# A hold behind the silu step in the build-time plan of a fused attention and SwiGLU kernel

## The chip, the cores and the metric

The kernel runs on one core of a Trainium2 chip. The core has a matrix engine (TensorE, PE in the profile, with its weight loads as PEld), a vector engine (VectorE, DVE), a scalar engine (ScalarE, ACT), GpSimd (POOL) and SyncE (SP), which here only issues DMAs. Each engine takes its own instructions strictly in the order in which they were emitted and waits on semaphores of the others. The metric is the device time of one execution in microseconds (us), less is better. The time before is the median of three runs, 379.68 us (379.57 to 379.87).

## The reference

Causal attention with a forget gate (64 heads of 576 tokens, 64 wide), whose output is laid out as 4608 tokens of 512, followed by a SwiGLU feed-forward block with 1536 hidden columns:

```python
scores = q @ k.T / sqrt(64) + (cum[:, None] - cum[None, :])   # cum = cumsum(log(clip(f, 1e-4, 1)))
attn   = softmax(where(causal, -1e9, scores))
x      = (attn @ v) -> (4608, 512)
g      = x @ w_gate
out    = (g * sigmoid(g) * (x @ w_val)) @ w_out
```

Inputs and output are float32; the kernel computes its matmuls in bf16.

## The kernel before

The kernel is not written as a fixed sequence. Every step (a matmul group, an activation, a DMA) is first recorded as an `Op` with its engine, an estimated duration, its predecessors, the buffers that it takes and releases, and a key. `Plan.run` then simulates the five engines at build time: whenever an engine is free, it takes the ready step with the smallest key whose buffers can be had, emits its instructions there and then, and moves that engine's clock on by the estimated duration. The order in which steps are emitted is the order in every engine's queue on the chip, DMA queues among them; the estimated times themselves are not in the program, only the order. So an estimate that changes by a tenth of a microsecond can let another step be the ready one, and from there on all queues may differ.

When a step ends in the plan, three events are pushed. The engine is free at `busy[e]`. Steps that can run only on the same engine learn of it at `busy[e]` too; steps of other engines learn of it later by `PIPE[e]` (0.12 us for VectorE, 0.2 for TensorE):

```python
o.done = end + self.PIPE[e]
push(busy[e], "wake", None)
push(o.done, "end", o)
push(busy[e], "done", (o, e, True))
push(o.done, "done", (o, e, False))
```

The attention part handles a pair of heads at a time: scores on TensorE (`score`, line 704), exponentials on ScalarE (`expo`, 738), the causal mask on GpSimd (`mask`, 747), weighing by V on TensorE (`weigh`, 761), then on VectorE the reciprocal of the row sums (`invert`, 768) and the scaling (`scale`, 773). A scaled pair goes into `xT`, through TensorE and a VectorE copy or by a DMA transpose on SP's queue (`cross`, 791). One PSUM bank ("o") holds the weighed sums of a head; the next head's weighing takes it when the scaling has released it. Loads of later batches are paced by fixed release times.

The feed-forward part runs over twelve token tiles, `TILES = (512, 512, 128) * 4` in effect, and in a 512-token tile over twelve blocks of 128 hidden columns. One such unit (`unit`, line 1057) is: gate matmuls into a bank (`gate`, 919), tanh on ScalarE (`tanh`, 930), silu on VectorE (`silu`, 940: (tanh + 1) times the gate bank, written to a `th` buffer), value matmuls into a second bank (919 with `wv`), and the product on VectorE (`times`, 943: `th` times the value bank, written to `hh`). Silu releases the gate bank, the product the value bank; four banks ("f") serve the feed-forward part until 290 us in the plan. A 128-token tile does the same for four blocks at once (`ffn1`, line 1099; `gate4` 926, `times4` 947, `pairs` 952, which sums what `times4` wrote). From tile 8 on, ScalarE computes silu by itself (`whole`, 933), and no VectorE silu exists: 82 of them run in tiles 0 to 7.

The products of a 512-token tile are summed in pairs on VectorE (`sums`, 976, three steps for each pair of blocks) and multiplied by the output weights with seven products in place of eight (`product`, 985); the weights' own sums are made once (`blend`, 964). The results go through ScalarE, GpSimd and VectorE (1011, 1018, 1022, 1043, 1046) into `ot` and to memory. The first tile uses a plain multiplication (`project`, 992), 128-token tiles `single` (998).

Keys decide among ready steps: tanh, silu, product and `pairs` have -5, attention steps some hundreds and thousands, feed-forward matmuls 100000 and more for each tile, the sums 50000 and the weights' sums 40000. A table `ORDER` overrides the keys of the steps numbered 0 to 596 and 1521 to 1580 (with gaps): the loads and the decay rows, the first batches of attention, and the first units of tile 0. Among steps with one key, the one recorded first goes first.

Of the kernel before, what the change touches and what calls it, by code (L numbers as in the profile page):

```python
# [34 lines left out]
class Plan:  # L35
# [9 lines left out]
    def op(self, eng, fn, after=(), behind=(), take=(), use=(), key=0.0, ready=0.0, dma=None):  # L45
        o = Op(eng, fn, list(after), behind, list(take), list(use), key, ready, dma)
        for b in o.use:
            b.left += 1
        self.ops.append(o)
        return o  # L50
# [26 lines left out]
    def run(self, idle=None):  # L77
# [9 lines left out]
        busy = {e: 0.0 for e in engines}  # L87
# [5 lines left out]
        left, t, seq = len(self.ops), 0.0, 0  # L93
        events = []

        def push(at, kind, o):
            nonlocal seq
            seq += 1
            heapq.heappush(events, (at, seq, kind, o))
# [9 lines left out]
        while left:  # L109
# [3 lines left out]
            t = events[0][0]  # L113
            while events and events[0][0] <= t + 1e-9:
                _, _, kind, o = heapq.heappop(events)
                if kind in ("queue", "dma"):
                    for r, share in shares():
                        r[0][0] -= (t - moved) * share
                        while r and r[0][0] < 1e-6:
                            over, n = r.pop(0)  # L120
# [27 lines left out]
                elif kind == "done":  # L148
                    o, e, own = o
# [6 lines left out]
            for e in engines:  # L156
                while busy[e] <= t + 1e-9:
                    k = kind_of.get(e)
                    full = k and lanes[k][taken[k] % 8] > t
                    if e == "SP" and full:  # L160
                        break
                    ready[e] = [o for o in ready[e] if o.start is None]
                    best = None
                    for o in sorted(ready[e], key=lambda o: (o.key, o.n)):
                        if o.dma is not None and full:
                            continue
                        if self._takes(o, t):
                            best = o
                            break
                    if best is None:  # L170
                        break
                    o = best
                    o.start, o.ran = t, e
                    dur = o.eng[e]
                    if e == "PE":
                        dur *= self.clock(t)
                        self._fill(idle, busy[e], t)
                    o.fn(e)
                    busy[e] = end = t + dur
                    for s in o.then:  # L180
                        s.wait -= 1
                        if not s.wait:
                            push(max(t, s.ready), "ready", s)
                    if o.dma is not None:
                        o.lane = taken[k] % 8
                        lanes[k][o.lane] = 1e9
                        taken[k] += 1
                        push(max(end + (0.53 if o.tag == "f" else 0.9), T_SW if e == "POOL" else 0.0), "queue", o)
                        push(busy[e], "wake", None)
                    else:  # L190
                        o.done = end + self.PIPE[e]
                        push(busy[e], "wake", None)
                        push(o.done, "end", o)
                        push(busy[e], "done", (o, e, True))
                        push(o.done, "done", (o, e, False))
        return max(o.done for o in self.ops)

# [24 lines left out]
def kernel(ctx, tc, q, k, v, f, w_gate, w_val, w_out, out):  # L222
# [11 lines left out]
    MT = 512  # L234
# [67 lines left out]
        lambda t: 2.0 if t < TWARM else 1.0,  # L302
    )

    def op(eng, fn, *args, tag=None, packet=20.0, **kw):
        if not isinstance(eng, dict):
            eng = {eng[0]: eng[1]}
        o = plan.op(eng, lambda e: fn(e, *args), **kw)
        o.tag, o.packet = tag, packet
        return o  # L310

    E = {"ACT": nc.scalar, "DVE": nc.vector, "POOL": nc.gpsimd, "SP": nc.sync, "PE": nc.tensor}
# [1 line left out]
    def act(n):  # L314
        return 0.055 + n / 1200

    def dve(n, psum=True):
        return (n + (75 if psum else 58)) / 960

    def mm(*cols):  # L320
        return sum(c / 2400 + 0.0025 for c in cols)
# [147 lines left out]
    def blank(e, what):  # L469
# [46 lines left out]
        else:  # L516
            if what != "rest":
                fill32(e, VB[what][:, :, :, D:].bitcast(F32), ONE2)
            if what:
# [4 lines left out]
              after=[op(("DVE", 0.07), lambda e: nc.vector.memset(warm, 1.0), key=-30)])  # L524
# [532 lines left out]
    def unit(t, fc, t0, n, hs, lo, kk, after):  # L1057
        if (t, fc) == ALONE:
            tabled.append(op(("ACT", 1.4), turn_table, after=before + exps, key=-6, tag="table"))
        needs = [o for a, b, done in x_ready.values() if a < t0 + n and b > t0 for o in done]  # L1060
        wr = [w_ready["g", fc // FCG], w_ready["v", fc // FCG]]
        bg, bv, bt = Buf(*F_POOLS(t)), Buf(*F_POOLS(t)), Buf("th")
        p, r = divmod(fc, 2)
        fresh = hs[p] is None
        if fresh:
            hs[p] = Buf("hh")
            hs[p].first = None
        g = op(("PE", mm(*[n] * KD)), gate, wg, fc, t0, n, bg, after=needs + wr + after, behind=[] if fresh else [hs[p].gate], take=[bg] + ([hs[p]] if fresh else []), key=kk, tag=("gp", t, fc))
        if fresh:
            hs[p].gate = g  # L1070
        alone = (t, fc) >= ALONE
        if alone:
            b = op(("ACT", act(n)), whole, n, bg, bt, after=[g] + tabled, take=[bt], use=[bg], key=-5, tag=("tanh", t, fc))
        else:
            b = op(("ACT", act(n)), tanh, n, bg, bt, after=[g], take=[bt], use=[bg], key=-5, tag=("tanh", t, fc))
            before.append(b)
            b = op(("DVE", dve(n)), silu, n, bg, bt, after=[b], use=[bg, bt], key=-5, tag=("silu", t, fc))
        a = op(("PE", mm(*[n] * KD)), gate, wv, fc, t0, n, bv, after=[g], take=[bv], key=kk + 1, tag=("vp", t, fc))
        m = op(("DVE", dve(n)), times, n, bv, bt, hs[p], r, lo, 1.0 if alone else 0.5, after=[a, b, hs[p].first],
               use=[bv, bt, hs[p]], key=-5, tag=("mul", t, fc))  # L1080
        if fresh:
            hs[p].first = m
        read.append((t0, t0 + n, [g, a]))
        return g, m
# [14 lines left out]
    def ffn1(t, t0):  # L1099
        key, bn, ms, first = 1e5 * (t + 1), Buf("nh"), [], []  # L1100
        for fq in range(KF // 4):
            if (t, 4 * fq) == ALONE:
                tabled.append(op(("ACT", 1.4), turn_table, after=before + exps, key=-6, tag="table"))
            needs = [o for a, b, done in x_ready.values() if a < t0 + P and b > t0 for o in done]
            wr = [w_ready[n, c] for n in "gv" for c in range(4 * fq // FCG, (4 * fq + 3) // FCG + 1)]
            bg, bv, bt = Buf(*F_POOLS(t)), Buf(*F_POOLS(t)), Buf("th")
            kk = key + 400 * fq
            g = op(("PE", mm(*[P] * 4 * KD)), gate4, wg, fq, t0, bg, after=needs + wr + [last_gate[0]], behind=first, take=[bg] + ([] if fq else [bn]), key=kk, tag=("gp", t, 4 * fq))
            first = first or [g]
            alone = (t, 4 * fq) >= ALONE  # L1110
            if alone:
                b = op(("ACT", act(MT)), whole, MT, bg, bt, after=[g] + tabled, take=[bt], use=[bg], key=-5, tag=("tanh", t, 4 * fq))
            else:
                b = op(("ACT", act(MT)), tanh, MT, bg, bt, after=[g], take=[bt], use=[bg], key=-5, tag=("tanh", t, 4 * fq))
                before.append(b)
                b = op(("DVE", dve(MT)), silu, MT, bg, bt, after=[b], use=[bg, bt], key=-5, tag=("silu", t, 4 * fq))
            a = op(("PE", mm(*[P] * 4 * KD)), gate4, wv, fq, t0, bv, after=[g], take=[bv], key=kk + 1, tag=("vp", t, 4 * fq))
            m = op(("DVE", dve(MT)), times4, fq, bv, bt, 1.0 if alone else 0.5, after=[a, b] + first, use=[bv, bt, bn], key=-5, tag=("mul", t, 4 * fq))
            ms.append(op({"DVE": fast(HALF)}, pairs, fq, after=[m], use=[bn], key=-5, tag=("pairs", t, fq)))
            read.append((t0, t0 + P, [g, a]))  # L1120
        last_gate[0] = g
        tails.append((t, t0, key, bn, ms))
# [129 lines left out]
    t0 = 0  # L1252
    for t, n in enumerate(TILES):
        ffn(t, t0, n) if n == MT else ffn1(t, t0)
        t0 += n
    for r in tails[:QUICK]:
        simple(*r)
    ready = [w_ready["o", c] for c in range(NCO)]
    blended = [op({e: f((KF // 2) * HALF // 2) + 0.35 * (n // 2 == 1) for e, f in BLEND_ON.items()}, blend, n, after=ready, key=BLEND_KEY + n, ready=BLEND_AT, tag=("blend", n)) for n in range(6)]
    blended += [op({e: f((KF // 2) * HALF // 2) for e, f in BLEND_ON.items()}, blend, n, after=blended[:6] + plain, key=BLEND_KEY + n, ready=BLEND_AT, tag=("blend", n)) for n in range(6, 10)]  # L1260
    for r in tails[QUICK:]:
        (finish if TILES[r[0]] == MT else lone)(*r, blended)

# [16 lines left out]


QUICK = 1
TILES = (512, 512, 128) * 3 + (512, 512, 128)


def F_POOLS(t):
    return ("f",) + tuple((x, WIDE_AT, 1e9) for x in "sot")
# [152 lines left out]
```

## Time and profile before

| | |
|---|---|
| median of three runs | 379.68 us |
| the profiled execution | 379.88 us |
| its span, first to last instruction | 378.1 us |
| granted TensorE clock | 1.000 |
| VectorE busy | 259.9 us |
| ScalarE busy | 213.3 us |
| GpSimd busy | 168.6 us |

In the profile, "L940" is line 940 of the kernel. A row of instructions in order of time gives the start, the duration, engine, line, operation, output and inputs with their shapes; a bracket at its end gives how long the engine had been idle before it and whose result ended that. A matmul's end is modelled, so a short wait of TensorE between two matmuls does not show as idle time. "th", "hh", "su", "nh", "ps" are the tiles of those names with their buffer numbers left out.

### The profile page before, as it was taken

What the parts mean: (1) busy time and instruction counts of PE and PEld (TensorE: products, weight loads), DVE (VectorE), ACT (ScalarE), POOL (GpSimd) and SP (SyncE); (2) the same over time, 40 slices, a digit from 0 to 9 for tenths busy, and PEclk for the clock granted to TensorE, in tenths of its full rate; (3) what the DMA queues carried; (4) which work ended last, traced back from release to release, by engine and by line L of the source; (5) the groups of instructions that cost most, each with busy time, mean ns of one, the idle gap of its engine ahead of it and who ended that gap; (6) DMA issues with size and microseconds to landing.
All of it is one profiled execution on the core that took longest, in us unless ns stands there. A gap on an engine that the chain in (4) does not pass through costs nothing.

```text
span 378.1 us, 9696 instructions
## 1 busy us (share of the span) xinstructions
PE 369.3 (98%) x3715; PEld 248.7 (66%) x3715; DVE 259.9 (69%) x605; ACT 213.3 (56%) x436; POOL 168.6 (45%) x396
## 2 busy tenths in 40 slices
PE   8899999999999999999999999999999999999996
PEld 5667655455679655775468965578666964584596
DVE  7879886499947699538983669854889246717633
ACT  7899953265646544766477465757775223323322
POOL 8897544135656243695058632656440400040021
PEclk9999999999999999999999999999999999999999
DMA  8999998895949998999969999497730120011012
GB/s 149 189 198 196 206 209 157 178 199 102 167 84 215 172 193 159 142 201 209 187 127 181 203 239 202 88 179 174 146 37 19 57 83 2 1 56 57 0 54 88
DMA packets 125179, 52.04 MB, mean 138 GB/s; under 512 B 111838, under 2 KB 119582, under 8 KB 124366
## 3 DMA queue, kind: packets, MB, share of 16 engines
q1 hardware_dynamic: 108638, 36.15, 48.7%
q0 software_dynamic: 16288, 15.14, 26.3%
q8 instruction: 29, 0.48, 0.5%
q10 hardware_dynamic: 208, 0.14, 0.1%
q14 instruction: 16, 0.13, 0.1%
HBM read 38.56 MB, written 17.07 MB: 147 GB/s over the span
## 4 chain that ended last, share of the span: by engine, by line
PE 87%; DVE 6%; DMA 2%; ACT 2%; issue 1%; POOL 0%; DVEq 0%; ACTq 0%; POOLq 0%
PE ps L919 40%; PE ps L985 16%; PE ps L704 9%; PE ps L761 8%; PE ps L926 5%; PE ps L998 3%; PE ps L992 3%; DVE hh L943 2%; DVE su L976 2%; DMA su<-in_q_dram 1%; DVE th L940 1%; DMA natv<-in_v_dram 1%; DVE xn L773 1%; PE ps L722 1%; PE ps L778 1%
## 5 line engine op out<-in xcount | busy, mean ns | idle before, releaser
L738 ACT ACTIVATE PT<-ps 128x384 bf16<-128x384 f32 (+2 forms) x192 | 90.9, 510 | 19.1 <-PE ps L704 12.6
L919 PE MATMUL ps<-xT,wv 128*128 128x512 bf16 (+1 forms) x400 | 99.3, 370 | 0.0
L919 PE MATMUL ps<-xT,wg 128*128 128x512 bf16 (+1 forms) x400 | 99.1, 370 | 0.0
L943 DVE SCALAR_TENSOR_TENSOR hh<-th,ps 128x512 bf16<-128x512 f32 (+1 forms) x100 | 66.2, 664 | 23.3 <-PE ps L919 16.3
L930 ACT ACTIVATE th<-ps 128x512 f32<-128x512 f32 (+1 forms) x82 | 47.2, 577 | 52.0 <-PE ps L919 45.1
L747 POOL TENSOR_SCALAR_AFFINE_SELECT PT<-PT 128x128 bf16<-128x128 bf16 (+1 forms) x192 | 53.7, 288 | 42.2 <-ACT PT L738 37.0
L704 PE MATMUL ps<-QK 68*128 68x256 bf16 x392 | 63.0, 261 | 0.0
L919 PEld LDWEIGHTS <-wg 128*128 128x128 bf16 x400 | 37.7, 97 | 34.5
L919 PEld LDWEIGHTS <-wv 128*128 128x128 bf16 x400 | 37.5, 97 | 34.5
L940 DVE SCALAR_TENSOR_TENSOR th<-th,ps 128x512 f32<-128x512 f32 (+1 forms) x82 | 53.5, 653 | 9.2 <-ACT th L930 8.8
L747 POOL TENSOR_SCALAR_AFFINE_SELECT PTa<-PTa 128x256 bf16<-128x256 bf16 x64 | 26.7, 419 | 69.6 <-ACT PTa L738 68.3
L976 DVE TENSOR_TENSOR su<-hh 128x512 bf16<-128x512 bf16 (+1 forms) x126 | 46.6, 413 | 1.1
L985 PEld LDWEIGHTS <-su 128*128 128x128 bf16 x420 | 40.1, 98 | 5.5 <-DVE su L976 0.4
L761 PE MATMUL ps<-VB,PT 128*128 128x65 bf16 x768 | 41.9, 193 | 0.0
L704 PEld LDWEIGHTS <-QK 68*128 68x128 bf16 x392 | 31.3, 97 | 12.9 <-ACT QK L328 0.2
L761 PEld LDWEIGHTS <-PT 128*128 128x128 bf16 x768 | 34.7, 97 | 7.5 <-POOL PT L747 0.6
L1018 POOL TENSOR_TENSOR ot<-ot 128x256 f32<-128x256 f32 x14 | 10.1, 722 | 63.7 <-ACT ot L1011 63.7
L933 ACT ACTIVATE th<-ps 128x512 f32<-128x512 f32 x30 | 17.9, 596 | 33.1 <-PE ps L919 27.7
L738 ACT ACTIVATE PTa<-ps 128x384 bf16<-128x384 f32 x64 | 30.9, 488 | 9.9 <-PE ps L704 8.7
L768 DVE RECIPROCAL rc<-ps 128x5 f32<-128x5 f32 (+2 forms) x68 | 12.7, 187 | 31.0 <-PE ps L761 30.8
L773 DVE TENSOR_TENSOR xn<-ps,rc 128x320 bf16<-128x320 f32 (+2 forms) x72 | 32.4, 453 | 2.2
L985 PE MATMUL ps<-wt,su 128*128 128x256 bf16 x252 | 33.2, 272 | 0.2 <-DVE su L976 0.2
(101 smaller groups left out, 410.4 us busy)
## 6 DMA issues: line engine op xcount, KB each, us to landing
out_dram<-ot SPq DMA_DIRECT2D x35, 256.0 KB
natv<-in_v_dram SPq DMA_DIRECT2D x25, 256.0 KB
qk_d<-in_q_dram POOLq DMA_DIRECT2D x24, 144.0 KB, 3.7
qk_d<-in_k_dram POOLq DMA_DIRECT2D x24, 144.0 KB, 4.7
wv<-in_moe_w_val_dram POOLq DMA_DIRECT2D x3, 512.0 KB, 9.8
wg<-in_moe_w_gate_dram POOLq DMA_DIRECT2D x3, 512.0 KB, 12.3
wo<-in_moe_w_out_dram POOLq DMA_DIRECT2D x4, 384.0 KB, 13.7
VB<-in_v_dram POOLq DMA_DIRECT2D x7, 128.0 KB, 10.0
```

The source lines that it names most:

```text
L704: nc.tensor.matmul(s[:, c : c + w], QK[:KR, hqk[p].i, 1, j * S + kt * P : j * S + (kt + 1) * P], QK[:KR, hqk[p].i, 0, j * S + q0 : j * S + ...
L738: nc.scalar.activation(place(h, i)[:, OFFS[i] : OFFS[i] + c], ps(bs)[:, :c], AF.Exp, scale=0.125)
L747: nc.gpsimd.affine_select(out=d, in_=d, pattern=pat, compare_op=ALU.is_ge, fill=0.0, base=0, channel_multiplier=-1,)
L761: nc.tensor.matmul(o[:, lo : lo + D + 1], pt[:, c : c + P], VB[hvb[b].i][:, kt, hb, : D + 1], start=first and n == 0, stop=last and n == l ...
L773: nc.vector.tensor_mul(XN[bx.i][:, qb : qb + nq, j], o, r)
L919: nc.tensor.matmul(ps(bf)[:, a:b], w[:, ko, fc * P : (fc + 1) * P], xT[:, ko, at : at + b - a], start=ko == 0 and a == 0, stop=ko == KD - ...
L926: nc.tensor.matmul(ps(bf)[:, c * P : (c + 1) * P], w[:, ko, (4 * fq + c) * P : (4 * fq + c + 1) * P], xT[:, ko, lo : lo + P], start=c + ko ...
L930: nc.scalar.activation(TH[bt.i][:, :n], ps(bf)[:, :n], AF.Tanh, scale=0.5)
L940: nc.vector.scalar_tensor_tensor(out=t, in0=t, scalar=1.0, in1=ps(bf)[:, :n], op0=ALU.add, op1=ALU.mult)
L943: nc.vector.scalar_tensor_tensor(out=HH[bh.i][:, r, lo : lo + n], in0=TH[bt.i][:, :n], scalar=by, in1=ps(bf)[:, :n], op0=ALU.mult, op1=ALU ...
L976: E[e].tensor_tensor(out=o, in0=x, in1=y, op=f)
L985: nc.tensor.matmul(ps(bf)[:, c * HALF : (c + 1) * HALF], left(g)[:, q * P : (q + 1) * P], right[:, g], start=opens and g == 0, stop=g == K ...
```

## The change

`op` takes a further argument, `raw`, 0 by default, and keeps it on the step. In `Plan.run`, the event that tells steps of the same engine of a step's end is pushed later by that amount; the engine itself is free when it was, and steps of other engines and buffers are told when they were. The two silu steps get `raw=RAW` with `RAW = 0.17`, and the product of the 128-token tiles gets `raw=0.1`. The product of the 512-token tiles, the reciprocal and all others keep 0. Keys, estimated durations, buffers and the computation of every step stay as they are. The instructions are the same; their order in the queues comes out of a plan in which a VectorE step that reads silu's result becomes ready 0.17 us behind silu's end, and `pairs` 0.1 us behind its product's.

```diff
@@ -191,7 +191,7 @@
                         o.done = end + self.PIPE[e]
                         push(busy[e], "wake", None)
                         push(o.done, "end", o)
-                        push(busy[e], "done", (o, e, True))
+                        push(busy[e] + o.raw, "done", (o, e, True))
                         push(o.done, "done", (o, e, False))
@@ -302,11 +302,11 @@
-    def op(eng, fn, *args, tag=None, packet=20.0, **kw):
+    def op(eng, fn, *args, tag=None, packet=20.0, raw=0.0, **kw):
         if not isinstance(eng, dict):
             eng = {eng[0]: eng[1]}
         o = plan.op(eng, lambda e: fn(e, *args), **kw)
-        o.tag, o.packet = tag, packet
+        o.tag, o.packet, o.raw = tag, packet, raw
         return o
@@ -1074,7 +1074,7 @@
-            b = op(("DVE", dve(n)), silu, n, bg, bt, after=[b], use=[bg, bt], key=-5, tag=("silu", t, fc))
+            b = op(("DVE", dve(n)), silu, n, bg, bt, after=[b], use=[bg, bt], key=-5, raw=RAW, tag=("silu", t, fc))
@@ -1113,9 +1113,9 @@
-                b = op(("DVE", dve(MT)), silu, MT, bg, bt, after=[b], use=[bg, bt], key=-5, tag=("silu", t, 4 * fq))
+                b = op(("DVE", dve(MT)), silu, MT, bg, bt, after=[b], use=[bg, bt], key=-5, raw=RAW, tag=("silu", t, 4 * fq))
...
-            m = op(("DVE", dve(MT)), times4, fq, bv, bt, 1.0 if alone else 0.5, after=[a, b] + first, use=[bv, bt, bn], key=-5, tag=("mul", t, 4 * fq))
+            m = op(("DVE", dve(MT)), times4, fq, bv, bt, 1.0 if alone else 0.5, after=[a, b] + first, use=[bv, bt, bn], key=-5, raw=0.1, tag=("mul", t, 4 * fq))
@@ -1280,6 +1280,7 @@
 QUICK = 1
+RAW = 0.17
```

## The prediction

> **What bounds the kernel now.** I read the page first: totals, then busy shares by slice (the rows here are total busy times, then TensorE in 40 slices).
>
> ```profile
> span 378.1 us, 9696 instructions
> PE 369.3 (98%) x3715; PEld 248.7 (66%) x3715; DVE 259.9 (69%) x605; ACT 213.3 (56%) x436; POOL 168.6 (45%) x396
> ...
> PE   8899999999999999999999999999999999999996
> ```
>
> TensorE (PE) is busy for 369.3 of 378.1 us. The other 8.8 us are all that any new order can win on it, and much of that lies in the first and the last slice. So the second view is busy time by stretches (columns: length, then PE, PEld, DVE, ACT, POOL busy with instruction counts, clock, DMA).
>
> ```profile
> 28.00:60.00 32.00, 32.00 (x339) 21.43 (x334) 27.86 (x60) 25.95 (x58) 19.56 (x50) 1.00 1.14 186
> 60.00:290.00 230.00, 227.19 (x2233) 150.61 (x2230) 166.88 (x360) 135.77 (x282) 112.23 (x281) 1.00 0.88 162
> 290.00:378.10 88.10, 85.17 (x697) 58.99 (x695) 43.38 (x93) 27.40 (x46) 11.93 (x12) 1.00 0.12 43
> ```
>
> The silu steps run between 29.88 and 291.11 us (rows below). Ahead of 60 us TensorE has no visible idle time; from 60 to 290 it has 230.00 - 227.19 = 2.81 us; what follows has no silu on VectorE, and its 2.93 us of idle time are the end of the program. The target is 2.81 us. The third view names those waits: TensorE's instructions in order of time, those with an idle bracket.
>
> ```profile
> 97.21 0.25 PE L761 MATMUL ps<-VB,PTa 128*128 128x65 bf16 x3 [0.81 <-DVE xn L773]
> 104.26 0.28 PE L985 MATMUL ps<-wo,hh 128*128 128x256 bf16 x1 [0.21 <-DVE hh L943]
> 105.25 0.94 PE L985 MATMUL ps<-wt,su 128*128 128x256 bf16 x7 [0.17 <-DVE su L976]
> 106.48 0.25 PE L761 MATMUL ps<-VB,PTa 128*128 128x65 bf16 x3 [0.28 <-DVE xn L773]
> 152.08 0.26 PE L761 MATMUL ps<-VB,PTa 128*128 128x65 bf16 x3 [0.17 <-POOL PTa L747]
> 155.08 0.25 PE L761 MATMUL ps<-VB,PTa 128*128 128x65 bf16 x3 [0.27 <-DVE xn L773]
> 193.71 0.25 PE L761 MATMUL ps<-VB,PTa 128*128 128x65 bf16 x3 [0.36 <-DVE xn L773]
> ```
>
> These add up to 2.27 us; the other 0.54 us are gaps too short to be named. Six of the seven end on VectorE (DVE), and four on the same thing: a head's weighing by V (L761) cannot open the one output bank until the softmax scaling of the head before (L773) has emptied it, and that scaling stands in VectorE's queue behind feed-forward work.
>
> **What the held step costs today.** VectorE's instructions in order of time, with the first and the last place where silu (L940) stands directly ahead of the product that reads it (L943), and a busy stretch between:
>
> ```profile
> 29.88 0.42 DVE L940 SCALAR_TENSOR_TENSOR th<-th,ps 128x256 f32<-128x256 f32 x1
> 30.40 0.42 DVE L943 SCALAR_TENSOR_TENSOR hh<-th,ps 128x256 bf16<-128x256 f32 x1
> ...
> 146.31 0.68 DVE L940 SCALAR_TENSOR_TENSOR th<-th,ps 128x512 f32<-128x512 f32 x1
> 147.09 0.69 DVE L943 SCALAR_TENSOR_TENSOR hh<-th,ps 128x512 bf16<-128x512 f32 x1
> 147.70 0.28 DVE L976 TENSOR_TENSOR su<-hh 128x256 bf16<-128x256 bf16 x1
> 147.90 0.68 DVE L940 SCALAR_TENSOR_TENSOR th<-th,ps 128x512 f32<-128x512 f32 x1
> 148.69 0.69 DVE L943 SCALAR_TENSOR_TENSOR hh<-th,ps 128x512 bf16<-128x512 f32 x1
> 149.41 0.76 DVE L976 TENSOR_TENSOR su<-hh 128x512 bf16<-128x512 bf16 x2
> ...
> 290.32 0.68 DVE L940 SCALAR_TENSOR_TENSOR th<-th,ps 128x512 f32<-128x512 f32 x1
> 291.11 0.69 DVE L943 SCALAR_TENSOR_TENSOR hh<-th,ps 128x512 bf16<-128x512 f32 x1
> ```
>
> Silu to its product is 147.09 - 146.31 = 0.78 us from start to start; the product to a step that does not read it is 147.70 - 147.09 = 0.61, with nearly the same duration on its row. So a dependent neighbour costs 0.17 us more, in which VectorE does nothing. In the whole list I count 69 adjacent pairs, 66 of them with this gap of about 0.10 between one's end and the other's start; behind 58 of the 66 the next VectorE step then starts without idle time, which I take as a sign that another step stood ready. The new constant is the same 0.17.
>
> The Trainium skill, "VectorE: DVE Perf Modes", section "The DRAIN you can't avoid", says that after every VectorE step the next one waits until the pipe is empty, and that leaving out semaphores between chained steps doesn't shorten that. Read strictly, 0.61 would not occur beside 0.78, and moving the product away would win nothing; the rows of this case contradict that reading (0.61 against 0.78), and by it the sum below would be 0 in place of 1.27 us.
>
> **The change part by part.** It removes no instruction and adds none: each engine's busy time stays as it is, only the order in the queues moves.
>
> 1. Silu's hold (0.17 us for its reader in the plan). At silu's end the plan used to take the product at once (key -5 outranks all but other -5 steps). Now any ready step may start in those 0.17 us, and the product follows. Each filled gap gives VectorE 0.17 us; 58 x 0.17 = 9.9 us over the run, nearly all of it on an engine that is not the bound.
> 2. The product of the 128-token tiles (0.1 us for `pairs`). Twelve such products exist, and a product to `pairs` is 212.45 - 211.73 = 0.72 us in the rows below, against 0.61 undisturbed: 12 x 0.11 = 1.3 us of VectorE at most. No named wait is preceded by them: 0.
>
> ```profile
> 211.73 0.69 DVE L947 SCALAR_TENSOR_TENSOR nh<-th,ps 128x512 bf16<-128x512 f32 x1 [3.11 <-PE ps L926]
> 212.45 0.29 DVE L952 TENSOR_TENSOR nh<-nh 128x256 bf16<-128x256 bf16 x1
> ```
>
> 3. What the held product costs. One step gets in ahead of it: a sum (147.70 to 147.90, 0.20 us; the larger form 0.76 / 2 = 0.38 at 149.41), a reciprocal (96.67 - 96.45 = 0.22, in item 4), or the next unit's silu (0.61). So it starts from 0.20 - 0.17 = 0.03 to 0.61 - 0.17 = 0.44 us later. Behind it wait the release of the value bank and the sums, and behind the bank the gate matmuls two units on. TensorE in the same stretch:
>
> ```profile
> 146.01 1.03 PE L919 MATMUL ps<-xT,wg 128*128 128x512 bf16 x4
> 146.87 1.03 PE L919 MATMUL ps<-xT,wv 128*128 128x512 bf16 x4
> 147.73 1.03 PE L919 MATMUL ps<-xT,wg 128*128 128x512 bf16 x4
> 148.60 1.03 PE L919 MATMUL ps<-xT,wv 128*128 128x512 bf16 x4
> ```
>
> Four banks serve two units. The product at 147.09 ends at 147.78 and frees a bank that the fourth group here needs at 148.60: 0.82 us to spare. The bank that silu frees at 146.99 is needed at 147.73: 0.74 to spare. A lateness of 0.03 to 0.44 us therefore stays hidden behind matmuls already queued: 0. If the cover is gone (two overtakings in a row, 0.88 us), each case costs 0.06 us; 35 places where a sum follows the pair would cost 2.1 us, the upper bound.
>
> 4. Where the 0.17 us arrive. VectorE's rows in order of time: the first and the last adjacent pair ahead of the largest wait with what follows it, and the silus that open and close the stretches ahead of the two others; then the busy times of the first stretch.
>
> ```profile
> 80.37 0.68 DVE L940 SCALAR_TENSOR_TENSOR th<-th,ps 128x512 f32<-128x512 f32 x1
> ...
> 95.06 0.67 DVE L940 SCALAR_TENSOR_TENSOR th<-th,ps 128x512 f32<-128x512 f32 x1
> 95.84 0.69 DVE L943 SCALAR_TENSOR_TENSOR hh<-th,ps 128x512 bf16<-128x512 f32 x1
> 96.45 0.19 DVE L768 RECIPROCAL rc<-ps 128x5 f32<-128x5 f32 x1
> 96.67 0.49 DVE L773 TENSOR_TENSOR xn<-ps,rc 128x320 bf16<-128x320 f32 x1
> ...
> 151.68 0.68 DVE L940 SCALAR_TENSOR_TENSOR th<-th,ps 128x512 f32<-128x512 f32 x1
> ...
> 179.75 0.68 DVE L940 SCALAR_TENSOR_TENSOR th<-th,ps 128x512 f32<-128x512 f32 x1
> ...
> 191.56 0.67 DVE L940 SCALAR_TENSOR_TENSOR th<-th,ps 128x512 f32<-128x512 f32 x1
> ...
> 80.00:98.00 18.00, 17.05 (x146) 9.56 (x144) 17.17 (x36) 11.88 (x26) 10.54 (x25) 1.00 0.85 146
> ```
>
> VectorE is busy for 17.17 of 18 us and shows no idle bracket there, so a saved 0.17 is handed on to all that stand behind. Seven adjacent pairs stand between 80.37 and 95.06: 7 x 0.17 = 1.19 us, more than the 0.81 that L761 waits at 97.21. The reciprocal itself may slip ahead of the product, but the scaling may not: by then the product is ready and outranks it. So of this pair alone the scaling gains about 0.2, and the rest has to come from the queue. Likewise seven pairs between 179.75 and 191.56 (1.19 us) against 0.36 at 193.71, and four between 146.31 and 151.68 (0.68 us) against 0.27 at 155.08. Ahead of 104 to 106.48 no pair stands adjacent: nothing there. Recoverable: 0.81 + 0.36 + 0.27 = 1.44 us; lower bound 0, if the queue is refilled by work that TensorE does not need. The evidence is nearer the upper end, since each wait has more gaps ahead of it than it needs; I take the filled share, 1.44 x 58/66 = 1.27 us.
>
> The sum: the profiled execution took 379.88 us (span 378.1 and 1.78 around it); 379.88 - 1.27 = 378.61. It stands 0.20 above the median of the runs, 379.68, so **378.4 us** against that median.
>
> **Rivals.**
>
> *The time is won and not felt.* VectorE gets its 0.17 us, but TensorE's order is redrawn too and meets as many short waits elsewhere. For it: the named waits are 2.27 us in 230, 1%, so anything may replace them. Against: the three waits share one cause. 379.7 us.
>
> *No gap to fill*, the strict reading of the page above, as a mechanism here: each step carries its 0.17 wherever it stands, the product only moves back. Its price by the rows is 0, or 379.7; 0.78 against 0.61 speaks against it. Or *the plan has nothing ready at silu's end* and keeps the pairs adjacent: also 379.7; 58 followers without idle time speak against that.
>
> *Slower: the early stage loses its fit.* Between 28 and 60 us TensorE shows 32.00 of 32 us busy although VectorE (27.86) and ScalarE (25.95) are both near full there: the exponentials, the bank evictions and the first tile's silus just mesh. The steps whose keys are listed one by one (0 to 596, 1521 to 1580) are mostly those of this stage and what feeds it; the first hold falls at 29.88 and from there each engine's queue is another. If that stage and the next attention stretch come to run like 80 to 120 us, where named waits are 0.81 + 0.21 + 0.17 + 0.28 = 1.47 in 40 us, TensorE loses that once more, and hidden gaps with it: 379.68 + 1.47 = 381.2 us. It decides from the point where TensorE shows idle time before 80 us. Against: nothing in the rows but the cover in item 3.
>
> *Slower: a batch's hand-over is missed.* POOL's cast of V waits for its load (waits by engine and line):
>
> ```profile
> POOL VB L330 <- DMA natv<-in_v_dram: 6.6, 3, 4.8
> PE ps L761 <- DVE xn L773: 1.7, 4, 0.8
> ```
>
> Today that 4.8 us wait is covered by feed-forward matmuls. Moved orders on SP (loads, transposes, stores in one queue) can make a load later, or spend the cover earlier. Half of 4.8 exposed gives 379.68 + 2.4 = 382.1 us.
>
> **How the numbers follow.** The forecast (378.4, its own range 377.4 to 378.9) has 0.40: the whole 2.27 us recovered gives 377.4. Not felt 0.14, no gap or nothing ready 0.05; early stage 0.27, hand-over 0.14. Some of the two slower ones and of the forecast would end near no change, so I give 0.39 for faster by over 0.2% (0.76 us, about what a measurement of this kernel can tell from no change), 0.20 for within it, 0.41 for slower. The range 377.3 to 382.0 leaves out a tenth on each side: above it half of the hand-over's share and a stall of both kinds, below it hidden gaps closed as well.
>
> **What would show it.** In the changed profile: fewer places where L943 stands 0.78 behind L940, with sums, reciprocals or silus between; VectorE's busy time unchanged; the waits of L761 for L773 under 0.5 us in total; TensorE's busy time in 28 to 60 us still full. I would be wrong if most pairs stay adjacent, if the four waits return at other places, if L919 begins to show idle time (banks released late), or if the waits on V's load grow.

## The result and the profile after

| | before | changed |
|---|---|---|
| median | 379.68 us (379.30 to 379.87, 5 runs) | 376.45 us (375.70 to 377.27, 5 runs) |
| span of the profiled execution | 378.1 us | 374.5 us |

The ratio is 0.9915, with a 95% interval of 0.9898 to 0.9932: 3.2 us faster, where 1.3 had been forecast, and below the range of the prediction. The span is 3.6 us shorter.

The page of the changed kernel, in the rows that answer to those of before:

```profile
span 374.5 us, 9689 instructions
PE 368.0 (98%) x3715; PEld 249.2 (67%) x3715; DVE 256.9 (69%) x605; ACT 212.5 (57%) x436; POOL 169.5 (45%) x396
...
PE   7899999999999999999999999999999999999996
```

The same 3715 matmuls are busy for 368.0 us in place of 369.3. So the span lost two things: idle time of TensorE (8.8 to 6.5 us) and 1.3 us that the page had counted as busy. VectorE's busy time fell by 3.0 us with the same 605 steps, where the prediction had expected it unchanged. The rows of independent neighbours overlap (below, a silu that starts at 89.42 and lasts 0.68 us, and a sum that starts at 90.02), and the page counts an overlap once; how much of the 3.0 us that makes is not worked out here. The busy times by stretches of the changed kernel:

```profile
28.00:60.00 32.00, 32.00 (x341) 21.60 (x336) 27.56 (x60) 25.89 (x58) 20.40 (x50) 1.00 1.16 189
60.00:290.00 230.00, 229.58 (x2276) 154.20 (x2273) 167.18 (x368) 137.20 (x284) 112.27 (x280) 1.00 0.92 162
290.00:374.50 84.50, 81.59 (x650) 55.66 (x647) 39.85 (x84) 25.22 (x43) 11.94 (x12) 1.00 0.12 45
```

The early stage stays without idle time, the end has the same 2.9 us, and between 60 and 290 us the idle time fell from 2.81 to 0.42 us. To see where the time came from, the same TensorE instructions are looked up in both traces. First before, then changed (the first group of the first 128-token tile, the group that follows it, the first of tile 5, the first of tile 8):

```profile
101.70 1.06 PE L926 MATMUL ps<-xT,wg 128*128 128x128 bf16 x16
117.01 1.06 PE L926 MATMUL ps<-xT,wv 128*128 128x128 bf16 x16
...
194.55 1.06 PE L926 MATMUL ps<-xT,wg 128*128 128x128 bf16 x16
...
290.03 1.06 PE L926 MATMUL ps<-xT,wg 128*128 128x128 bf16 x16
```

```profile
100.11 1.06 PE L926 MATMUL ps<-xT,wg 128*128 128x128 bf16 x16
114.29 1.06 PE L926 MATMUL ps<-xT,wv 128*128 128x128 bf16 x16
...
191.06 1.06 PE L926 MATMUL ps<-xT,wg 128*128 128x128 bf16 x16
...
286.46 1.06 PE L926 MATMUL ps<-xT,wg 128*128 128x128 bf16 x16
```

The lead is 1.59 us at tile 2's start, 2.72 at its second group, 3.49 at tile 5 and 3.57 at tile 8, and it stays there to the end. Three quarters were won by 117 us, in and right behind the stretch in which VectorE had no idle time.

What happened on VectorE shows in two places of that kind. A silu, one 512-wide sum and a product before, and the same three in the changed kernel (VectorE in order of time):

```profile
226.04 0.68 DVE L940 SCALAR_TENSOR_TENSOR th<-th,ps 128x512 f32<-128x512 f32 x1
226.82 0.69 DVE L943 SCALAR_TENSOR_TENSOR hh<-th,ps 128x512 bf16<-128x512 f32 x1
227.43 0.42 DVE L976 TENSOR_TENSOR su<-hh 128x512 bf16<-128x512 bf16 x1
227.76 0.68 DVE L940 SCALAR_TENSOR_TENSOR th<-th,ps 128x512 f32<-128x512 f32 x1
```

```profile
89.42 0.68 DVE L940 SCALAR_TENSOR_TENSOR th<-th,ps 128x512 f32<-128x512 f32 x1
90.02 0.41 DVE L976 TENSOR_TENSOR su<-hh 128x512 bf16<-128x512 bf16 x1
90.35 0.68 DVE L943 SCALAR_TENSOR_TENSOR hh<-th,ps 128x512 bf16<-128x512 f32 x1
90.95 0.62 DVE L976 TENSOR_TENSOR su<-hh 128x512 bf16<-128x512 bf16 x2
```

227.76 - 226.04 = 1.72 us became 90.95 - 89.42 = 1.53. The durations are the same; the 0.19 us were the start that the product could not make. Of the 69 adjacent pairs 37 are left, and 30 of those show the gap.

### The profile page after: what moved, and what is told of

The parts are those of the page before. It is cut to its first block, busy times and chain, and to the rows that moved or that the text cites. A ratio compares the mean times of both kernels' runs of the same rounds, so it can differ in the third digit from the quotient of the medians.

```text
span 374.5 us, 9689 instructions
## 1 busy us (share of the span) xinstructions
PE 368.0 (98%) x3715; PEld 249.2 (67%) x3715; DVE 256.9 (69%) x605; ACT 212.5 (57%) x436; POOL 169.5 (45%) x396
## 4 chain that ended last, share of the span: by engine, by line
PE 93%; ACT 3%; DVE 2%; issue 1%; POOL 0%; DVEq 0%; ACTq 0%
PE ps L919 43%; PE ps L985 17%; PE ps L704 10%; PE ps L761 8%; PE ps L926 6%; PE ps L998 3%; PE ps L992 3%; PE ps L722 1%; PE ps L579 1%; PE ps L778 1%; ACT PT L738 1%; ACT QK L328 1%; PE ps L730 0%; ACT xT L363 0%; ACT PTa L738 0%
## 5 line engine op out<-in xcount | busy, mean ns | idle before, releaser
L747 POOL TENSOR_SCALAR_AFFINE_SELECT PT<-PT 128x128 bf16<-128x128 bf16 (+1 forms) x192 | 54.6, 291 | 41.6 <-ACT PT L738 35.9
L747 POOL TENSOR_SCALAR_AFFINE_SELECT PTa<-PTa 128x256 bf16<-128x256 bf16 x64 | 26.9, 423 | 63.9 <-ACT PTa L738 62.9
L761 PE MATMUL ps<-VB,PT 128*128 128x65 bf16 x768 | 41.4, 193 | 0.1
L761 PEld LDWEIGHTS <-PT 128*128 128x128 bf16 x768 | 34.1, 97 | 7.0 <-POOL PT L747 1.0
L773 DVE TENSOR_TENSOR xn<-ps,rc 128x320 bf16<-128x320 f32 (+2 forms) x72 | 32.4, 453 | 2.1
L1011 ACT ACTIVATE ot<-ps 128x512 f32<-128x512 f32 x28 | 16.7, 597 | 27.9 <-PE ps L985 26.5
```

The source lines that it names most:

```text
L747: nc.gpsimd.affine_select(out=d, in_=d, pattern=pat, compare_op=ALU.is_ge, fill=0.0, base=0, channel_multiplier=-1,)
L761: nc.tensor.matmul(o[:, lo : lo + D + 1], pt[:, c : c + P], VB[hvb[b].i][:, kt, hb, : D + 1], start=first and n == 0, stop=last and n == l ...
L773: nc.vector.tensor_mul(XN[bx.i][:, qb : qb + nq, j], o, r)
```

## The experiments

Each ratio stands against the kernel before on the same chip. "Pairs" counts the places of VectorE's queue where silu stands directly ahead of its product.

| run | pairs | median us | ratio, 95% interval |
|---|---|---|---|
| changed kernel | 37 | 376.45 | 0.9915 (0.9898 to 0.9932) |
| e1, step put between, other queues as before | 37 | 377.39 | 0.9937 (0.9925 to 0.9950) |
| e2, product put back, other queues as changed | 70 | 377.89 | 0.9955 (0.9943 to 0.9967) |
| e3, estimate alone | 63 | 377.59 | 0.9950 (0.9938 to 0.9962) |
| e4, holds of 0.002 us | 43 | 376.60 | 0.9923 (0.9909 to 0.9936) |
| e5, before redrawn | 69 | 379.63 | 0.9989 (0.9981 to 0.9998) |
| e6, before, GpSimd estimate moved | 69 | 380.11 | 1.0001 (0.9991 to 1.0010) |
| e7, before, TensorE's signal moved | 69 | 380.45 | 1.0005 (0.9992 to 1.0017) |
| e8, changed redrawn | 41 | 378.08 | 0.9943 (0.9931 to 0.9955) |
| e9, e1 in tile 1 only | 60 | 378.11 | 0.9958 (0.9943 to 0.9973) |
| e10, e1 elsewhere only | 46 | 379.22 | 0.9983 (0.9970 to 0.9996) |
| e11, before redrawn | 64 | 380.48 | 1.0022 (1.0009 to 1.0035) |
| e12, one more hold | 31 | 375.78 | 0.9897 (0.9875 to 0.9918) |
| e13, e3 redrawn | 66 | 379.87 | 1.0002 (0.9985 to 1.0018) |
| e14, e3 redrawn | 68 | 377.73 | 0.9955 (0.9941 to 0.9968) |
| e15, changed redrawn | 41 | 376.13 | 0.9910 (0.9896 to 0.9924) |
| e16, without the 0.1 us hold | 30 | 376.43 | 0.9918 (0.9904 to 0.9931) |

Three theories were set against each other. **Fill**: the gap behind silu is work time of VectorE, and a step put into it lets all that stands behind come earlier. **Fit**: the plan now knows the chip's clock better, and TensorE's order suits it. **Redraw**: the order of before was a poor draw, and most others are better.

### VectorE's queue alone, and all others alone (e1, e2)

The plan's emission is recorded, and one queue is edited before it is written out:

```diff
-                    o.fn(e)
+                    self.said.append((o, e, lambda o=o, e=e: o.fn(e)))
...
+            if kinds[0] == "silu":
+                x, y = said[n1][0], said[n2][0]
+                if fill and kinds[1] == "mul" and o in x.after and y.start - x.start < FILL:
+                    held, over = set(spot(x)), [p for p, _, _ in said[n1 + 1 : n2 + 1] if p is not None]
+                    if not any(x in p.after or x in p.behind or held & set((b.pool, b.i) for b in p.take) for p in over):
+                        said.insert(n2, said.pop(n1))
```

`n`, `n1`, `n2` are three VectorE steps in a row. e2 does the reverse on the changed plan: where `n2` is the product, it is moved to `n1`.

> The plan of before, with one thing done to its result: where silu stands directly ahead of its product in VectorE's queue and the next VectorE step is independent and follows within 0.75 us in the plan, that step is put between them. Adjacent pairs fall from 69 to 37, the number of the changed kernel; the queues of the four other engines are those of before, instruction for instruction. Theory 'fill' (the 0.17 us are won in VectorE's queue itself): most of the 3.2 us, 376.5 to 377.7 us, and the waits of L761 for L773 (1.7 us) mostly gone. Theory 'fit' (the plan's clock comes nearer to the chip's, so TensorE's order suits it better): little, 379.0 to 379.7. Theory 'redraw' (any new order would have done): no forecast but near 379.7, since nothing of TensorE's order is redrawn.

> The reverse: the plan of the changed kernel, and in its VectorE queue each product moved back directly behind its silu where its value matmuls were emitted before the step between. Adjacent pairs rise from 37 to 70; the four other queues are those of the changed kernel. Fill: most of the gain is gone, 378.5 to 380 us, and waits of TensorE on VectorE come back between 80 and 160 us. Fit and redraw: the gain stays, 376.3 to 377.2.

e1 came to 0.9937, 2.4 of the 3.2 us, with TensorE's queue the same instruction for instruction. That is won by VectorE's order alone, and redraw cannot make it. The order of the other queues is worth something too: e2, with 70 adjacent pairs, still has 0.9955, between the range of fill and that of the two other theories. Its waits of TensorE on the scaling come to the 1.7 us of before, but not at the same places: the one at 97.21 is gone, and the longest stands behind 150 us (a row by engine and line, then one of TensorE in order of time; the recording adds 38 lines, so L799 is L761 and L811 is L773):

```profile
PE ps L799 <- DVE xn L811: 1.7, 3, 1.0
```

```profile
151.63 0.25 PE L799 MATMUL ps<-VB,PTa 128*128 128x65 bf16 x3 [1.04 <-DVE xn L811]
```

The two gains, 2.4 and 1.7 us, come to 4.1, more than the 3.2 of the change. In part they remove the same waits, that at 97.21 above all: one by an earlier scaling, the other by other TensorE work ahead of it. The intervals of e1 and of the changed kernel overlap (from 0.9925 to 0.9932), so how much the other queues add to e1's gain is not shown.

### One busy stretch against the rest (e9, e10)

The edit of e1 with the further condition `70 < x.start < 105` in plan time, or its opposite: 9 places, all in tile 1, and 24.

> As the swap run, but only the nine places that the plan has between 70 and 105 us (tile 1, where VectorE had no idle time before): 9 x 0.17 = 1.5 us of VectorE. If that one busy stretch carries most of the gain, 377.8 to 378.5 us, with tile 2 (first L926 row, 101.70 us before) starting 1 us or more earlier or the stretch up to 120 us shortened by that. If the gain is spread evenly over the places, 9 of 33, 379.0 to 379.3.

> The other 24 places of the swap run, 24 x 0.17 = 4.1 us of VectorE. If the stretch of tile 1 carries most, 378.8 to 379.4 us. If spread evenly, 377.9 to 378.3. The two together should come to the 2.16 us of the swap run.

Nine places win 1.6 us (1.0 to 2.2 by the interval), 0.18 for each. The other 24 win 0.65 us (0.2 to 1.1), 0.03 for each. So the moves pay where VectorE has work back to back and TensorE waits behind it, and hardly elsewhere. That the 0.18 comes near the 0.17 which each place frees is chance, as the rows at the end of this section show. The stretch from 80 to 120 us, e9 and then e10:

```profile
80.00:120.00 40.00, 39.92 (x459) 29.49 (x458) 30.93 (x71) 25.73 (x55) 25.61 (x61) 1.00 0.85 157
```

```profile
80.00:120.00 40.00, 38.37 (x407) 26.95 (x406) 31.76 (x68) 24.92 (x53) 24.23 (x57) 1.00 0.79 149
```

With nine steps moved, TensorE is busy for 39.92 of those 40 us; without them its idle time is 1.63 us, close to the 1.61 us of before (0.81, 0.21, 0.17 and 0.28 named, the rest too short for it). e9 shows the price of a held product too:

```profile
77.47 1.02 PE L957 MATMUL ps<-xT,wv 128*128 128x512 bf16 x4 [0.28 <-DVE hh L981]
```

L957 is the value matmuls' line 919 and L981 the product's 943: here a value bank came 0.28 us late by the bracket. In the changed kernel no such wait is listed.

The moves also did something that no theory had named. VectorE before, from the scaling that ended the wait at 97.21 to the one that ended the wait at 106.48, with the longest step between, then GpSimd before (L330 is its cast of V, L747 the mask):

```profile
96.67 0.49 DVE L773 TENSOR_TENSOR xn<-ps,rc 128x320 bf16<-128x320 f32 x1
...
100.57 2.23 DVE L976 TENSOR_TENSOR su<-hh 128x512 bf16<-128x512 bf16 x1
...
105.93 0.49 DVE L773 TENSOR_TENSOR xn<-ps,rc 128x320 bf16<-128x320 f32 x1
```

```profile
100.73 1.17 POOL L330 CAST VB<-natv 128x512 bf16<-128x512 f32 x2
101.86 0.29 POOL L747 TENSOR_SCALAR_AFFINE_SELECT PT<-PT 128x128 bf16<-128x128 bf16 x1
102.11 0.40 POOL L747 TENSOR_SCALAR_AFFINE_SELECT PTa<-PTa 128x256 bf16<-128x256 bf16 x1
102.47 0.48 POOL L747 TENSOR_SCALAR_AFFINE_SELECT PT<-PT 128x128 bf16<-128x128 bf16 x1
```

VectorE in e9, from the same scaling to the same (L1014 is the sums' line 976), then the second weighing on TensorE:

```profile
95.52 0.48 DVE L811 TENSOR_TENSOR xn<-ps,rc 128x320 bf16<-128x320 f32 x1
...
99.11 0.85 DVE L1014 TENSOR_TENSOR su<-hh 128x512 bf16<-128x512 bf16 x1
...
100.48 0.70 DVE L1014 TENSOR_TENSOR su<-hh 128x256 bf16<-128x256 bf16 x1
...
103.65 0.49 DVE L811 TENSOR_TENSOR xn<-ps,rc 128x320 bf16<-128x320 f32 x1
```

```profile
104.19 0.25 PE L799 MATMUL ps<-VB,PTa 128*128 128x65 bf16 x3
```

A 512-wide sum, 0.42 us at 227.43, lasted 2.23 us here while GpSimd worked without a pause. In e9 it lasted 0.85 us, and the next sum 0.70. From the one scaling to the other VectorE needed 105.93 - 96.67 = 9.26 us before and 103.65 - 95.52 = 8.13 us in e9, with the same steps in the same order; all nine places lie ahead of the first scaling. TensorE's weighings follow the start of these scalings by 0.53 to 0.55 us in both kernels (97.21 and 106.48 before; 104.19 in e9, and 96.05 in a row further below), so between them TensorE went at VectorE's pace. About 1.1 us of e9's gain therefore come from the shorter sums, and about 0.5 us are left for the gaps themselves, after what the held product cost. The nine moves shifted the sums against GpSimd's work; nothing in the plan aims at that, and why a sum is stretched beside that work no run shows.

### Does a plan that only knows the time win? (e3, e4, and the redraws e5 to e8, e11, e13 to e15)

```diff
e3   op(("DVE", dve(n) + 0.17), silu, ...)      # both silu steps, no hold
e4   RAW = 0.002, raw=0.002                     # in place of 0.17 and 0.1
e5   act(n): 0.058 + n / 1200                   # in place of 0.055; e8 and e13 the same on the changed kernel and on e3
e6   pool(n): 0.125 + n / 1000                  # in place of 0.12
e7   PIPE "PE": 0.205                           # in place of 0.2
e11  act(n): 0.052 + n / 1200                   # e14 and e15 the same on e3 and on the changed kernel
```

> The kernel before with the estimate of each silu 0.17 us longer and no hold: the plan's VectorE is busy through the gap, so it knows the time but nothing can be put into it (63 adjacent pairs are left). Fill: no gain, 379 to 380.5 us. Fit: the gain, 376 to 377.5.

> The changed kernel with holds of 0.002 us in place of 0.17 and 0.1: a step that is ready at silu's end goes ahead of the product (43 adjacent pairs are left), but the plan's clock is that of before, and nothing that becomes ready later in the gap gets in. Fill: most of the gain, 376.5 to 377.8 us. Fit: 379 to 380.

> The kernel before with the fixed part of each ScalarE estimate 0.003 us longer: far less than any gap at issue, no hold, all 69 pairs left adjacent; only the draw of the order changes. Redraw (the order of before was a poor draw, and most others are better): 376.5 to 378.5 us. Fill and fit: within 1 us of before on either side, 378.7 to 380.5.

> The kernel before with the fixed part of each GpSimd estimate 0.005 us longer, no hold, 69 pairs adjacent: a second draw. Redraw: 376.5 to 378.5 us. Fill and fit: 378.7 to 380.5.

> The kernel before with TensorE's results seen by other engines 0.005 us later in the plan, no hold, 69 pairs adjacent: a third draw. Redraw: 376.5 to 378.5 us. Fill and fit: 378.7 to 380.5.

> The changed kernel with the ScalarE estimate of the jitter run 0.003 us longer (41 adjacent pairs): the hold stays, the order is drawn anew. Fill and fit: 375.5 to 377.5 us. Redraw: anything between 376 and 380.

> The kernel before with the fixed part of each ScalarE estimate 0.003 us shorter, no hold (64 adjacent pairs): a draw that changes TensorE's queue in twice as many rows as the change does. Redraw: 376.5 to 378.5 us. Fill and fit: 378.7 to 381.

> The fit-only kernel (silu's estimate 0.17 us longer, no hold, 66 adjacent pairs) with the fixed part of each ScalarE estimate 0.003 us longer. If the fit wins by itself: 376.8 to 378.4 us, as its first draw (377.6). If that was a lucky draw: 379 to 381, as the redraws of before.

> The same with the ScalarE estimates 0.003 us shorter (68 adjacent pairs). Fit: 376.8 to 378.4 us. Lucky draw: 379 to 381.

> The changed kernel with the ScalarE estimates 0.003 us shorter (41 adjacent pairs). Fill and fit together: 375.5 to 378.2 us, and below the fit-only draw with the same ScalarE estimates. If only luck tells them apart, no order between the two.

e4 wins 2.9 of the 3.2 us although its plan keeps the clock of before: who goes first at silu's end matters, not the 0.17 itself. Its TensorE queue is nearly that of before (some 30 of 3715 matmuls stand at another place), so most of the gain needs no new order there. e3 was a surprise, 0.9950 with 63 pairs left adjacent, and 377.59 us lies just above what fit had forecast. Two more draws settle part of it. By the ScalarE constant (0.052, 0.055, 0.058), the ratios are 1.0022, 1, 0.9989 without any of it, 0.9955, 0.9950, 1.0002 with the estimate alone, and 0.9910, 0.9915, 0.9943 with the hold. The hold is ahead of both in each of the three. The estimate alone wins in two draws and nothing in the third; whether fit has an effect of its own is left open. As an account of the whole gain redraw falls: e1 wins with TensorE's queue untouched, and e5 and e11, which change some 2600 and 2000 rows of that queue (old and new rows counted, weight loads included, buffer numbers left out) where the change itself changes 976, move the time by 0.1 and 0.2%, in either direction. But e3 and e14 win 1.9 and 1.7 us with hardly a gap filled, so an order can be worth that much, for whatever reason. e6 and e7 turned out to be weak tests, since TensorE's queue hardly changed (not at all, and by some 60 rows), and e8 missed its upper bound by 0.6 us.

The stretched sum sorts these kernels. In the traces the longest sum lasts 1.49 to 2.47 us in the seven kernels with a ratio above 0.998 (before, e5, e6, e7, e10, e11, e13), and 0.85 to 1.19 us in the eleven others, e3 and e14 among them. So a fourth account stands beside fill and fit: part of each gain is a sum that no longer falls into GpSimd's work. No run moved that alone, and it is not the whole: in e10 the sum still takes 2.23 us, and the kernel wins 0.65 us.

e11 shows a redraw that keeps the cause (TensorE's waits by engine and line):

```profile
PE ps L761 <- DVE xn L773: 2.8, 5, 0.8
...
PE ps L985 <- DVE su L976: 0.9, 1, 0.9
```

### The second hold, and one hold more (e16, e12)

```diff
e16 -   ... key=-5, raw=0.1, tag=("mul", t, 4 * fq))
e16 +   ... key=-5, raw=0.0, tag=("mul", t, 4 * fq))
e12 -               use=[bv, bt, hs[p]], key=-5, tag=("mul", t, fc))
e12 +               use=[bv, bt, hs[p]], key=-5, raw=0.12, tag=("mul", t, fc))
```

> The changed kernel without the 0.1 us hold behind the product of the 128-token tiles. The prediction costed that hold at nothing: 376.0 to 377.2 us, within a draw's spread of the changed kernel.

> The changed kernel with one more hold, 0.12 us behind the product of the 512-token tiles for the sums that read it (0.72 against 0.60 us from start to start in the trace of before), to see whether a better one is near. Fill and fit together: 375.5 to 376.5 us, 0 to 1 us under the changed kernel; TensorE has only 0.4 us of named waits left there between 60 and 290 us, so not much more. Redraw: anything between 376 and 380.

Without the hold of the 128-token tiles the time is the changed kernel's (376.43 against 376.45 us). With a hold behind the other products as well, 375.78 us is the lowest median of all, but its interval (0.9875 to 0.9918) overlaps that of the changed kernel, so a further gain is not shown.

## Why the prediction was right and where it failed

The forecast of 378.4 us had the direction and the place, and less than half of the size: 1.27 us off the profiled execution, where the medians differ by 3.2.

**The mechanism was right, and not the only one.** The 0.17 us behind silu is a gap that an independent step fills, the reading that no gap exists fell (1.72 against 1.53 us for the same three steps), and the wait of L761 for L773 went from 1.7 us to nothing that the waits by engine and line list. The Trainium skill, "VectorE: DVE Perf Modes", section "The DRAIN you can't avoid", taken strictly, would have left e1 at the time of before; it came to 0.9937. The same section goes on: "A next op that is not held starts earlier". The strict reading left that sentence out, and the rows agree with it: the sum at 147.70 starts before the row of the product ahead of it ends (147.09 and 0.69 us), while a product behind its silu starts 0.10 us after silu's end. What stands there of the semaphore's cost was not tried here.

**The place was right and drawn too small.** Item 4 named the stretch ahead of 97.21; e9 shows that moving steps in this stretch alone is worth 1.6 us. But the item gave nothing to the waits from 104 to 106.48, since no pair stands adjacent right ahead of them. They are gone as well, also in e9, which moves nothing behind 96 us. The item looked for adjacent pairs and not at how long VectorE's other steps take: what made VectorE late there was in large part the sum of 2.23 us at 100.57, and in e9 VectorE passed that stretch in 1.13 us less with nothing moved in it. In the changed kernel the lead grew from 1.59 to 2.72 us between tile 2's first group and its second, 1.13 us for waits that were put down at 0. Its longest sum there lasts 1.17 us; how those 1.13 us divide between the shorter sum and the closed gaps is not shown.

**The size of a wait was read too small.** The term that failed here is "0.81 + 0.36 + 0.27 = 1.44". A bracket begins at a matmul's modelled end, and that lies behind the point where TensorE could have gone on. TensorE before, at two of the three waits:

```profile
95.86 0.55 PE L704 MATMUL ps<-QK 68*128 68x256 bf16 x4
97.21 0.25 PE L761 MATMUL ps<-VB,PTa 128*128 128x65 bf16 x3 [0.81 <-DVE xn L773]
...
192.32 1.03 PE L919 MATMUL ps<-xT,wv 128*128 128x512 bf16 x4
193.71 0.25 PE L761 MATMUL ps<-VB,PTa 128*128 128x65 bf16 x3 [0.36 <-DVE xn L773]
```

and the same kinds of group in the changed kernel, undisturbed:

```profile
95.32 0.55 PE L704 MATMUL ps<-QK 68*128 68x256 bf16 x4
95.70 1.03 PE L919 MATMUL ps<-xT,wv 128*128 128x512 bf16 x4
96.57 0.26 PE L761 MATMUL ps<-VB,PTa 128*128 128x65 bf16 x3
```

Behind the scores the next group starts after 0.38 us, behind the value matmuls after 0.87; before, it was 1.35 and 1.39. The waits were 0.97 and 0.52 us, and the brackets said 0.81 and 0.36: 0.16 were hidden each time. With 0.16 for each of the seven named waits, an estimate from these two, TensorE lost 2.27 + 1.12 = 3.39 us, close to the 3.6 us by which the span fell; the three of item 4 alone come to 1.44 + 0.48 = 1.92. So the sum of the prediction failed in three terms: 1.44 us where these three waits cost about 1.92, nothing for waits worth 1.13, and a factor of 58/66 although all three waits are gone. The hidden 0.16 us are also why TensorE's "busy" time fell by 1.3 us with the same matmuls, and why the 377.4 of the prediction, all named waits gone, was no bound.

The largest of these waits can be followed in e9, whose TensorE queue is that of before (L742 is the scores' line, L799 the weighing's). First TensorE, then the reciprocal that stood behind a product before (L806 is 768):

```profile
95.64 0.55 PE L742 MATMUL ps<-QK 68*128 68x256 bf16 x4
96.05 0.25 PE L799 MATMUL ps<-VB,PTa 128*128 128x65 bf16 x3
```

```profile
94.84 0.20 DVE L806 RECIPROCAL rc<-ps 128x5 f32<-128x5 f32 x1 [0.38 <-PE ps L799]
```

1.35 us became 0.41, and VectorE, which had no idle time in that stretch, now waits 0.38 us for TensorE: it has caught up. The changed kernel has that and in addition another order on TensorE, with the value matmuls (95.70) ahead of the weighing.

**The filled share of 58/66** was no good price either. What counts is not how many gaps are filled but whether TensorE waits behind them: 0.18 us for a place in tile 1, more than half of it from the shorter sums, and 0.03 elsewhere.

**The held product** was put at nothing, up to 2.1 us. In e1 and e9, where TensorE's order cannot answer, it costs one wait of 0.28 us by its bracket; in the changed kernel none shows.

**The rivals.** The early stage kept its fit in this draw (32.00 of 32 us busy). A missed hand-over did not appear: no wait of TensorE for a load of V is listed, and GpSimd's own waits for it, 6.6 us before, are 6.8 us. Gains that nobody feels are what e10 shows, but only outside the busy stretch. Weighing the slower cases at 0.41 came from the thought that any new order is a risk of 1 to 2 us; the two large redraws of before measured that risk at 0.1 and 0.2%; the draws of e3 lie 0.5% apart, so it is not nothing, but no draw came out slower than before by more than those 0.2%.

## What to carry to other kernels

Where one engine's queue is full for some ten microseconds and the busiest engine waits behind it, look for a dependent neighbour's gap, as a start-to-start time longer than that of the same step ahead of an independent one, and count only the places in such a stretch. Don't multiply the gap by the places: a move also shifts all that follows against the other engines, and here that was worth more than half of what nine moves won. Follow the late engine to where it catches up, not to the next wait, and look on the way for steps that last longer than their like. And take TensorE's waits from start to start against an undisturbed group of the same kind, since the idle bracket leaves out what lies under a modelled end.

## What the runs showed of the hardware that had not been expected

A named wait of TensorE was 0.16 us longer than its bracket at both places where it could be compared (0.97 against 0.81 us, 0.52 against 0.36). A 512-wide bf16 sum on VectorE, 0.42 us elsewhere, lasted 2.23 us while GpSimd cast and masked without a pause, and 0.85 us when the moves had shifted it. And redrawing some 2000 and more rows of the queue of TensorE, counted as above, moved the kernel before by 0.1 to 0.2% only, while moving nine VectorE steps past one neighbour each, with every other queue the same, moved it by 0.4%.
